# Weight decoding with a one-source 16-bit shift, reordered first loads and last tile, and a new planned order

## The chip, the cores and the metric

One core of one Trainium2 chip runs the whole program. The metric is the device time of one launch in microseconds (us). The runs of the kernel before took 1172.53, 1173.43 and 1179.7 us; their median, 1173.43 us, is the time before.

## The reference: attention, then two dense blocks

The inputs are q, k and v of shape (4, 12, 448, 64) in float32, two gain vectors, and four weight matrices in float64.

```
q_n = q / sqrt(mean(q*q) + 1e-6) * g_q        # the same for k with g_k
attn = softmax(q_n @ k_n^T / sqrt(64))
x = (attn @ v), heads joined                   # 1792 x 768
h = x @ w_in;   x = (h * sigmoid(1.702 h)) @ w_out         # 768 -> 2048 -> 768
h = x @ w_in2;  out = (h * clip(h + 3, 0, 6) / 6) @ w_out2 # 768 -> 2048 -> 768
```

[...] 

## The kernel before: tiles, stages and who sets the order

The work has these stages. For each of the four batches: normalise q and k, turn them (a transposing DMA), scores, exponentials, the product with v; then the first block's input product (`add_in1`) and output product (`add_out1`). The normalising and attention of a batch (`add_norm`, `add_units`) run beside the first block of the batch before it. After the four batches the second block runs over two chunks of 896 tokens in visits (`Quad`, `Visit`); the sum of the output is kept in `acc` and stored in the last visit of each chunk.

The order within each engine's queue is not written by hand. Each step is an `op` with a duration, its dependences and the engines that could do it; `Plan.order` simulates the engines with these durations and picks, for each engine, the ready step of highest rank. `CFG` holds the planner's numbers: biases between engines, look-ahead, offsets of the rank by group of steps, spacing of loads (`pw`, `pu`, `pv`), and `abias`, a penalty in ns that a DMA pays in the choice between the queue of ScalarE (ACT) and that of SyncE (SP). The emitted queues are in order: an instruction that waits holds what is behind it.

Decoding a piece of weight (`Weight.decoded`, line 550, for the first block; `Units.add`, line 703, for the second). A float64 is two 32-bit words. Four steps after its load:

- `sign`, on POOL (GpSimd), lines 578 and 722: the high word, read as float32, is multiplied to a signed zero, which leaves the sign bit in the result.
- `decode_a`, on DVE (VectorE), lines 585 and 728: the low word shifted right by 29 is or-ed into the result. It reads two tensors, in 32-bit words.
- `rebias`, on POOL or ACT, lines 569, 574, 734 and 739: the high word times 2^-112, in place.
- `decode_b`, on DVE, lines 592 and 743: the high word shifted left by 3 is or-ed into the result.

A piece is 128x768 words (W1 and both weights of the second block) or 128x1024 (W2). There are 60 `decode_a`: 16 for W1, 12 for W2 and 32 for the second block.

The start: `gains()` (line 510) is emitted before the planned order. It loads g_q and g_k on SP, sets constants on POOL and computes the joint gain on DVE (lines 518 to 524). The plan then begins with the loads of q and k, the squares (line 921), sums (924), the root (953 to 968), the gain on k (927), the norms (978), the float16 parts (984, 466, 996, 999) and the transposes (1022). The first tile of v for `add_head0` (line 1072) is loaded over the place of g_q, so its load waits until line 518 has read it.

The end: `Visit.leave` (line 1731) does 24 matmuls for one tile of 128 tokens, alternating between its two halves of 384 columns, then adds each half to `acc` on DVE (line 1749), and two DMAs store 64 rows each (line 1763).

Of the kernel before, what the change touches and what calls it, by code (L numbers as in the profile page):

```python
# [13 lines left out]
I64 = mybir.dt.int64  # L14
AF = mybir.ActivationFunctionType
# [18 lines left out]
    bias=[3440, 0, 1020, 1120, 7840],  # L34
    pw=[418, 636, 204686, 5498710540],
    pn=[8287, 2708, 4378, 1393],
    ps=[2095, 0, 1428, 193],
# [4 lines left out]
    look=[60, 250, 0, 0, 200],  # L42
    off=[-975, 86366, 127438, 91083, -33011, 29732, -19700, 94471, -29918, 18727, -18701, -18103, 48010, -34477, -678250, -4593, -16054, -152410, 41835, 254511],
    abias=1455,
    cuts=[],
    bias0=[680, 0, 510, 0, 6780],
    bias1=[4840, 1020, 6000, 730, 1800],
    dlook=1671,
    warm=9,
    late=789,  # L50
    idle=1000,
    pu=10770,
    pmost=5,
    pv=0,
    early_k=[0, 0, 0, 0],
    beside=0.9,
)
# [104 lines left out]
class Plan:  # L162
# [3 lines left out]
    def op(self, ways, deps=(), takes=None, gives=None, dma=None):  # L166

        if isinstance(ways, tuple):
            ways = [ways]
        o = Op(ways, deps, takes, gives, dma)  # L170
        o.key, o.off, o.bias = len(self.ops), self.off, self.bias
        self.ops.append(o)
        return o
# [37 lines left out]
    def order(self):  # L211
# [3 lines left out]
        dma_free = gen_free = seq_free = begun = 0.0  # L215
# [10 lines left out]
        for _ in self.ops:  # L226
            best = None
            for e in range(5):
                can = []
                for o in wait[e]:  # L230
                    r = o.ready[e]
                    if o.takes:
                        free_at = [l.ring.when(l, sum(m.ring is l.ring for m in o.takes[:i])) for i, l in enumerate(o.takes)]
                        if None in free_at:
                            continue
                        r = max([r] + [f[0] + CFG['late'] * (e == PE) for f in free_at])
                    if o.dma and len(o.ways) > 1:
                        r = max(r, dma_free - o.dma[2] - CFG['dlook'])
                    if len(o.ways) > 1:
                        ends = {w[0]: max(seq_free if o.dma and w[0] == ACT else free[w[0]], o.ready[w[0]], r) + w[1]  # L240
                                + (CFG['abias'] * (w[0] == ACT) if o.dma else o.bias[w[0]]) for w in o.ways}
                        if ends[e] > min(ends.values()):
                            continue
                    can.append((max(seq_free if o.dma and e == ACT else free[e], r), -o.rank, o.key, o))
                if can:
                    soon = min(can)[0] + LOOK[e]
                    c = min((c for c in can if c[0] <= soon), key=lambda c: c[1:3])
                    if best is None or c[:3] < best[0]:
                        best = (c[:3], c[3], e)
# [67 lines left out]
def attention_moe_moe_kernel(ctx, tc, q, k, v, g_q, g_k, w_in1, w_out1, w_in2, w_out2, out):  # L317
# [183 lines left out]
    gm, ge = small(), small()  # L501
# [8 lines left out]
    def gains():  # L510
        nc.sync.dma_start(out=gq_t, in_=g_q.unsqueeze(0).to_broadcast([128, D]))
        nc.sync.dma_start(out=gp, in_=g_k.unsqueeze(0).to_broadcast([128, D]))
        nc.gpsimd.memset(one, 1.0)
        make_identity(nc, ident)
        nc.gpsimd.tensor_copy(ident16, ident)
        for i in range(4):
            nc.gpsimd.memset(carve(gt, 7168 + 5376 * i, [128, 21, 128], F16)[:, 14:21, D:128], 0.0)
        nc.vector.tensor_tensor(out=gp, in0=gp, in1=gq_t, op=ALU.mult)
        nc.vector.tensor_reduce(out=gm, in_=gp, axis=AX.X, op=ALU.max, apply_absolute_value=True)
        exponent(ge, gm)  # L520
        nc.vector.reciprocal(gm, ge)
        nc.vector.tensor_scalar_mul(gp, gp, gm)
        nc.vector.tensor_single_scalar(out=alpha, in_=ge, scalar=2.0 ** -25, op=ALU.mult)
        nc.vector.tensor_single_scalar(out=nalpha, in_=ge, scalar=-(2.0 ** -25), op=ALU.mult)


    class Weight:
# [22 lines left out]
        def decoded(self, src, raw, cl):  # L550
# [21 lines left out]

            def rebias_act():
                nc.scalar.activation(out=high(), in_=high(), func=AF.Copy, scale=2.0 ** -112)

# [5 lines left out]

            def decode_a():
# [111 lines left out]
    class Units:  # L694
# [8 lines left out]
        def add(self, q, after, free):  # L703
# [7 lines left out]
            for j in range(2):  # L711
# [14 lines left out]
                def decode_a(cj=cj, wide=wide):  # L726
                    cu = cj.bitcast(U32)
                    nc.vector.scalar_tensor_tensor(
                        out=cu, in0=wide(U32)[:, :, 0], scalar=29, in1=cu,
                        op0=ALU.logical_shift_right, op1=ALU.bitwise_or,  # L730
                    )

                def rebias_pool(high=high):
                    nc.gpsimd.tensor_scalar(
                        out=high(), in0=high(), scalar1=2.0 ** -112, scalar2=1.0, op0=ALU.mult, op1=ALU.mult
# [23 lines left out]
                if self.wide:  # L759
                    x = op((POOL, t_pool(n), sign), [o] + ends[:1], takes=None if j else lease)  # L760
                    x = op((DVE, t_dve_bits(n), decode_a), [x])
                    o = op([(POOL, t_pool(n), rebias_pool), (ACT, t_act(n), rebias_act)], [x])
# [130 lines left out]
    def add_norm(bt, after):  # L893
# [8 lines left out]
        def sums_of(n):  # L902
# [13 lines left out]
            for i, src in ((0, q), (1, k)):  # L916
# [24 lines left out]
                if i:  # L941
                    bt.gained = op(two(gain), [o])
# [87 lines left out]
        for grp in groups:  # L1030
# [3 lines left out]
                (DVE, 1900, lambda n=grp[0], m=m: root(n, m)), sum((p[1] for p in parts), [])  # L1034
# [29 lines left out]
    def add_head0(bt, n, h, pieces, deps):  # L1064
# [5 lines left out]
        for p0, j0, j1, t0, t1, step in ((0, 0, 3, 0, 5, 2), (64, 0, 3, 1, 6, 2), (64, 3, 4, 6, 7, 1)):  # L1070
# [3 lines left out]
            loads.append(sp(64 * (j1 - j0) * 512, load, loads[:1], takes=None if loads else raw_l, wide=False))  # L1074
# [614 lines left out]
    class Visit:  # L1689
# [18 lines left out]
        def enter(self, tb, banks, some):  # L1708
# [3 lines left out]
            for i in some:  # L1712
                f = (0, 2, 1, 3)[i]

                def emit(i=i, f=f):
                    g = self.gview()
                    for j, (ge, we) in enumerate(((0, 0), (0, 1), (1, 0))):
                        for h in range(2):
# [8 lines left out]
                    (PE, t_mm(half, 6), emit), [last[0], W4.done[q]] + [self.done[f, s] for s in sides],  # L1727
                    takes=None if i else banks,
                )

        def leave(self, tb, acc_free, banks=None):
# [3 lines left out]
            if banks is None:  # L1735
                banks = [Lease(mm_ring, 1, True, both=not i) for i in range(2)]
                self.enter(tb, banks, (0, 1))
            self.enter(tb, banks, (2, 3))
            self.left_ = [last[0]]
            ends = []  # L1740
            for h in range(2):
# [11 lines left out]
                if part == 0:  # L1753
                    o = op((ACT, t_act(half, 1), first), [last[0], self.sized] + acc_free, gives=banks[h])
                else:
                    o = op((DVE, t_add(half), add), [last[0], added[at, h]], gives=banks[h])
                added[at, h] = o
                ends.append(o)
            if part == PARTS - 1:
                for i in range(2):  # L1760
                    def store(i=i):
                        b_, t = divmod(2 * at + i, TB)
                        queue().dma_start(out=orow[b_, t], in_=acc[64 * i:64 * i + 64, at])

                    sp(64 * DM * 4, store, ends, wide=False)
# [17 lines left out]
    b0 = batches[0]  # L1783
    off(0)
    add_norm(b0, [])
# [116 lines left out]
    with tc.manual_schedule():  # L1902
        gains()
# [41 lines left out]
```

## Time and profile before

| | before |
|---|---|
| median of 3 runs | 1173.43 us |
| the profiled execution | 1179.83 us |
| its span, first to last instruction | 1178.0 us |
| mean granted TensorE clock | 0.986 |
| busy: PE, DVE, ACT, POOL | 1078.3, 859.4, 716.3, 318.3 us |

PE is TensorE's matmuls, DVE VectorE, ACT ScalarE, POOL GpSimd, SP SyncE, which issues DMAs. A share of busy time is a mean over stages that are bound by different engines, so the rows below are mostly cut by stage. The matmuls of the profile overlap, and their ends are modelled.

### The profile page before, as it was taken

To read this page: it belongs to the slowest core of one execution; us is meant where nothing else is said; L and a number is where in the kernel's file an instruction comes from. 1 tells how busy PE (TensorE), PEld (TensorE's weight loads), DVE (VectorE), ACT (ScalarE), POOL (GpSimd) and SP (SyncE) were. 2 spreads that over 40 slices of the span, in tenths; PEclk is the share of its full clock that TensorE was granted. 3 is DMA by queue.
4 is the path that set the end of the run, shared out by engine and by line. 5 is a ranking of instruction groups with operands and counts; after the bars stand their busy time and mean duration, and the time that the engine had idled before them with its cause. 6 is when DMAs were issued, how large, how long until landed. Compare 5 with 4: busy or idle time off the path is not lost.

```text
span 1178.0 us, 18000 instructions
## 1 busy us (share of the span) xinstructions
PE 1078.3 (92%) x6590; PEld 594.2 (50%) x6590; DVE 859.4 (73%) x1497; ACT 716.3 (61%) x1507; POOL 318.3 (27%) x280
## 2 busy tenths in 40 slices
PE   2788898779989999999989999989999999999998
PEld 0555543345544455545545555445555555555554
DVE  6988889999879866598666888693648855935342
ACT  3989768888767989679885655463545332622210
POOL 5867735444423100140000324340002101100000
PEclk9899999979999999999999999999999999999999
DMA  6886477989758997689975427613423351213033
GB/s 170 202 222 164 157 200 203 186 190 264 148 155 220 193 200 154 153 217 192 194 154 137 158 76 262 223 67 150 127 92 108 107 165 32 76 51 114 1 87 101
DMA packets 236552, 178.88 MB, mean 152 GB/s; under 512 B 194864, under 2 KB 220208, under 8 KB 234928
## 3 DMA queue, kind: packets, MB, share of 16 engines
q1 hardware_dynamic: 227008, 160.86, 54.1%
q10 hardware_dynamic: 9456, 16.88, 4.8%
q8 instruction: 51, 0.84, 0.3%
q14 instruction: 37, 0.30, 0.1%
HBM read 97.88 MB, written 34.41 MB: 112 GB/s over the span
## 4 chain that ended last, share of the span: by engine, by line
PE 44%; DVE 22%; ACT 14%; DMA 11%; issue 5%; POOL 2%; SPq 1%; ACTq 0%; DVEq 0%; POOLq 0%
PE s L1604 8%; PE mm L1719 8%; PE s L1719 7%; PE mm L1604 6%; PE mm L1428 5%; PE mm L1360 5%; ACT p L1166 5%; DMA xt<-p 4%; DMA p<-in_v_dram 4%; DVE p L481 3%; ACT p L466 2%; DVE smalls L1161 2%; DVE gt L481 2%; PE mm L1081 2%; DVE smalls L924 2%
## 5 line engine op out<-in xcount | busy, mean ns | idle before, releaser
L1360 PE MATMUL mm<-xt,wa 128*128 128x448 f16 x1152 | 226.1, 354 | 7.3 <-DVE st L1409 4.1
L1428 PE MATMUL mm<-gt,wb 128*128 128x448 f16 x1152 | 226.2, 353 | 0.0
L1719 PEld LDWEIGHTS <-gt 128*128 128x128 f16 x1344 | 131.9, 98 | 98.7 <-issue 10.7
L1360 PEld LDWEIGHTS <-wa 128*128 128x128 f16 x1152 | 112.8, 99 | 111.0 <-issue 9.9
L1428 PEld LDWEIGHTS <-wb 128*128 128x128 f16 x1152 | 111.7, 98 | 104.1 <-issue 1.4
L1604 PEld LDWEIGHTS <-xt 128*128 128x128 f16 x1008 | 98.6, 98 | 94.6 <-issue 5.0
L1166 ACT ACTIVATE p<-s,smalls 128x448 f32<-128x448 f32 x168 | 120.8, 720 | 14.4 <-DVE p L481 5.2
L1604 PE MATMUL s<-wa,xt 128*128 128x448 f16 x621 | 122.6, 352 | 2.7 <-DVE st L1619 1.5
L481 DVE SCALAR_TENSOR_TENSOR p<-p,smalls 128x448 f16<-128x448 f32 x108 | 78.1, 749 | 25.9 <-ACT p L466 25.5
L1153 PE MATMUL s<-gt 128*128 128x448 f16 (+1 forms) x192 | 61.9, 366 | 37.0 <-ACT p L1166 35.6
L1161 DVE TENSOR_REDUCE smalls<-s 128x2 f32<-128x896 f32 (+1 forms) x96 | 91.7, 964 | 1.2 <-PE s L1156 1.1
L466 ACT ACTIVATE p<-p,smalls 128x448 f16<-128x448 f32 (+2 forms) x119 | 75.6, 669 | 22.2 <-DMA xt<-p 11.2
L1604 PE MATMUL mm<-wa,xt 128*128 128x448 f16 x387 | 76.6, 352 | 1.9 <-ACT wb L1626 1.9
L1719 PE MATMUL mm<-p,gt 128*128 128x384 f16 x372 | 72.3, 326 | 0.0
L722 POOL TENSOR_SCALAR wr<-wr 128x768 f32<-128x768 f32 x16 | 19.9, 1241 | 169.7 <-DVE xt L687 134.2
L1719 PE MATMUL s<-p,gt 128*128 128x384 f16 x300 | 61.0, 326 | 4.1 <-ACT wb L1626 2.6
L1719 PE MATMUL s<-gt 128*128 128x384 f16 x324 | 58.7, 333 | 3.4 <-DVE wb L1749 2.4
L1156 PE MATMUL s<-gt 128*128 128x448 f16 (+1 forms) x192 | 61.6, 362 | 0.0
L1719 PE MATMUL mm<-gt 128*128 128x384 f16 x348 | 60.8, 326 | 0.0
L1114 PE MATMUL mm<-xt,gt 128*64 128x64 f16 (+3 forms) x858 | 51.6, 265 | 4.3 <-DMA xt<-p 3.6
L1215 PE MATMUL mm<-gt,p 128*128 128x128 f32 x336 | 46.1, 293 | 9.5 <-ACT xt L1225 4.1
L481 DVE SCALAR_TENSOR_TENSOR gt<-st,smalls,gt 128x448 f16<-128x448 f32 x64 | 51.2, 808 | 4.5 <-ACT gt L466 4.2
(212 smaller groups left out, 1808.7 us busy)
## 6 DMA issues: line engine op xcount, KB each, us to landing
wr<-in_moe_w_in_dram SPq DMA_DIRECT2D x27, 768.0 KB, 4.9
wa<-park_x SPq DMA_DIRECT2D x21, 672.0 KB, 4.0
wr<-in_moe_w_out_dram SPq DMA_DIRECT2D x16, 768.0 KB, 4.5
qkd<-xt SPq DMA_DIRECT2D x18, 672.0 KB, 5.1
wr<-in_moe_w_out_dram SPq DMA_DIRECT2D x8, 1024.0 KB, 5.4
p<-in_v_dram SPq DMA_DIRECT2D x36, 224.0 KB, 3.8
park_x<-wa SPq DMA_DIRECT2D x2, 2688.0 KB, 12.1
out_dram<-wb SPq DMA_DIRECT2D x28, 192.0 KB, 2.6
```

Source lines behind the costliest of these rows:

```text
L466: nc.scalar.activation(out=dst(), in_=src(), func=AF.Copy, scale=s)
L481: nc.vector.scalar_tensor_tensor(out=dst(), in0=src(), scalar=s, in1=high(), op0=ALU.mult, op1=ALU.subtract)
L1114: nc.tensor.matmul(mm_t[ml.slot][64 * h:64 * h + 64, c:c + m * w], lhsT=vhl[:, 2 * (i % 4) + i // 4, part], rhs=pt[:, s:s + w, i, q0:q0 + ...
L1153: nc.tensor.matmul(o, lhsT=x[:, 64 * t:64 * t + m], rhs=x[:, 448:896], start=True, stop=False)
L1156: nc.tensor.matmul(o, lhsT=x[:, 64 * t:64 * t + m], rhs=x[:, 896:1344], start=False, stop=True)
L1161: nc.vector.tensor_reduce(out=nb, in_=s_t[sl.slot][:, :m, :S], axis=AX.X, op=ALU.max)
L1166: nc.scalar.activation(out=p(i), in_=s_t[sl.slot][:, i, :S], func=AF.Exp, bias=nb[:, i:i + 1], scale=alpha, accum_out=z[:, i:i + 1],)
L1215: nc.tensor.matmul(mm_t[tl.slot][:, 128 * j:128 * j + 128], lhsT=p(i)[:, c:c + 128], rhs=diag(), start=True, stop=True,)
L1360: nc.tensor.matmul(mm_t[ml.slot][:, :n], lhsT=w.inw(we, kc, f), rhs=x[:, xe, kc, :n], start=(kc == k0 and i == 0), stop=(kc == k1 - 1 and ...
L1428: nc.tensor.matmul(mm_t[ml.slot][:, :S], lhsT=W2.outw(we, fc, d * 128, 128), rhs=gv[:, ge_, fc, :], start=(fc == g.part.start and i == 0), ...
L1604: nc.tensor.matmul(self.bank(k), lhsT=w[:, we, fa, kc], rhs=xs[:, fb, xe, kc], start=first and kc == 0 and j == 0, stop=kc == 2 and j == 2 ...
L1719: nc.tensor.matmul(mm_t[banks[h].slot][:, :half], lhsT=g[:, ge, f, tb * 128:tb * 128 + 128], rhs=w4_t[part % 2][:, f, we, h * half:h * hal ...
```

## The change

`decode_a` becomes a shift of 16-bit words: of the four 16-bit words of a float64 it takes the second lowest, shifts it right by 13, and writes the low 16-bit word of each result. It reads one tensor, no longer the result. The value is the same, since the step `sign` has left zeros there. `sign` may now also be a 16-bit "and" on DVE, and `rebias` may also run on DVE; the planner chooses. The planner's duration for `decode_a` goes from 1.04 n + 150 ns to 0.72 n + 80 ns.

`gains()` is split. Constants are still emitted first. A one-element `Exp` on ACT comes first in the plan (`table`). The loads of g_q and g_k are planned DMAs, the arithmetic is a planned DVE step, and the gain on k and the first v load name it as a dependence. In the last tile of the last visit each half of 384 columns does its 12 matmuls by itself, is added as soon as its own are done, and is stored by two DMAs of its own (four of 64x384). The planner's numbers are new, `abias` goes from 1455 to 44617, its DMA model starts at 4800 ns, and a table `own` shifts the rank of some 80 single steps.

```diff
-    look=[60, 250, 0, 0, 200],
-    off=[-975, 86366, 127438, ...
-    abias=1455,
+    look=[0, 130, 60, 920, 540],
+    off=[-9158, 408922, -29895, ...
+    abias=44617,
...
-    pu=10770,
+    pu=419,
...
+    own={
+        1: 18285, 2: 13033, 4: 14353, 7: 16590, 17: 60615, 21: 15124, 23: 56483, 26: 34835, 28: 63794, 29: 27563,
...
+    def constants():
         nc.gpsimd.memset(one, 1.0)
         make_identity(nc, ident)
...
+    def table():
+        nc.scalar.activation(out=tab, in_=one, func=AF.Exp)
+
+    def load_gq():
+        queue().dma_start(out=gq_t, in_=g_q.unsqueeze(0).to_broadcast([128, D]))
+
+    def load_gk():
+        queue().dma_start(out=gp, in_=g_k.unsqueeze(0).to_broadcast([128, D]))
...
+    def low16(c):
+        return c.bitcast(U16).rearrange("p (n t) -> p n t", t=2)[:, :, 0]
+
+    def high16(c):
+        return c.bitcast(U16).rearrange("p (n t) -> p n t", t=2)[:, :, 1]
+
+    def last16(raw):
+        return raw.bitcast(U16).rearrange("p (n t) -> p n t", t=4)[:, :, 3]
+
+    def next16(raw):
+        return raw.bitcast(U16).rearrange("p (n t) -> p n t", t=4)[:, :, 1]
...
+            def sign_dve():
+                nc.vector.tensor_single_scalar(
+                    out=high16(c32()), in_=last16(wr_t[raw.slot][:, :n]), scalar=0x8000, op=ALU.bitwise_and
+                )
+
             def decode_a():
 
-                cu = c32().bitcast(U32)
-                nc.vector.scalar_tensor_tensor(
-                    out=cu, in0=wide(U32)[:, :, 0], scalar=29, in1=cu,
-                    op0=ALU.logical_shift_right, op1=ALU.bitwise_or,
+                nc.vector.tensor_single_scalar(
+                    out=low16(c32()), in_=next16(wr_t[raw.slot][:, :n]), scalar=13, op=ALU.logical_shift_right
                 )
...
-                x = op((POOL, t_pool(n), sign), [o], takes=cl)
-                x = op((DVE, t_dve_bits(n), decode_a), [x])
-                o = op([(POOL, t_pool(n), rebias_pool), (ACT, t_act(n), rebias_act)], [x])
+                x = op([(POOL, t_pool(n), sign), (DVE, t_fast(n), sign_dve)], [o], takes=cl)
+                x = op((DVE, t_fast(n), decode_a), [x])
+                o = op([(POOL, t_pool(n), rebias_pool), (ACT, t_act(n), rebias_act), (DVE, t_fast(n), rebias_dve)], [x])
...
-                    bt.gained = op(two(gain), [o])
+                    bt.gained = op(two(gain), [o] + with_gains)
...
-            loads.append(sp(64 * (j1 - j0) * 512, load, loads[:1], takes=None if loads else raw_l, wide=False))
+            loads.append(sp(64 * (j1 - j0) * 512, load, loads[:1] or with_gains, takes=None if loads else raw_l, wide=False))
...
+            final = self.turn + 1 == len(order) and tb + 1 == 2 * self.n // 128
+            made = [None, None]
+            if final:
+                banks = [Lease(mm_ring, 1, True) for _ in range(2)]
+                for h in range(2):
+                    self.enter(tb, banks, range(4), [h])
+                    made[h] = last[0]
...
-                for i in range(2):
-                    def store(i=i):
+                for i in range(4 if final else 2):
+                    def store(h=i // 2, i=i % 2):
                         b_, t = divmod(2 * at + i, TB)
...
+    op((ACT, 1400, table)).off = 1e9
     off(0)
+    with_gains = [op((DVE, 1500, gains), [sp(128 * 256, load_gq, wide=False), sp(128 * 256, load_gk, wide=False)])]
...
     with tc.manual_schedule():
-        gains()
+        constants()
         plan.run()
```

The second block's decoding is changed in the same way, with the same four new steps.

## Rows read from the trace of the kernel before

**Rows 1.** Page, part 1: busy us (share of the span) and instructions of each engine.

```profile
PE 1078.3 (92%) x6590; PEld 594.2 (50%) x6590; DVE 859.4 (73%) x1497; ACT 716.3 (61%) x1507; POOL 318.3 (27%) x280
```

**Rows 2.** Windows by stage: length, then busy us of PE, PEld, DVE, ACT, POOL; clock, DMA.

```profile
0.00:20.40 20.40, 0.00 (x0) 0.00 (x0) 11.56 (x34) 6.54 (x11) 9.95 (x19) 1.00 0.55 189
20.40:60.00 39.60, 30.68 (x168) 18.27 (x169) 38.21 (x61) 31.34 (x80) 33.72 (x30) 0.90 0.85 189
60.00:152.00 92.00, 77.70 (x553) 51.51 (x552) 76.07 (x123) 77.05 (x203) 66.56 (x57) 0.99 0.63 179
...
176.00:300.00 124.00, 102.12 (x645) 52.92 (x644) 118.98 (x198) 103.67 (x233) 56.84 (x41) 0.93 0.92 210
...
365.00:640.00 275.00, 265.17 (x1808) 140.79 (x1806) 202.49 (x395) 222.69 (x534) 36.87 (x38) 1.00 0.84 183
...
740.00:800.00 60.00, 53.24 (x296) 28.67 (x295) 46.06 (x83) 32.78 (x51) 22.73 (x20) 1.00 0.43 150
...
905.00:945.00 40.00, 37.56 (x211) 21.09 (x210) 32.30 (x50) 16.15 (x24) 6.79 (x6) 0.96 0.31 99
```

**Rows 3.** Waits of PE in 150 to 300 us: us in total, times, longest.

```profile
PE s L1153 <- ACT p L1166: 18.6, 11, 5.1
```

**Rows 4.** Timeline of the first 20 us: start, duration, engine, line, operation.

```profile
0.74 0.41 ACTq L918 DMA_DIRECT2D wb<-in_q_dram  x1
...
6.64 0.23 DVE L518 TENSOR_TENSOR gp<-gp,p 128x64 f32<-128x64 f32 x1 [6.64 <-DMA gp<-in_g_k_dram]
6.90 0.71 ACTq L1072 DMA_DIRECT2D p<-in_v_dram  x1
...
7.64 1.28 ACT L921 ACT_TABLE_LOAD   x1 [7.64 <-DVE smalls L440]
...
8.94 2.91 ACT L921 ACTIVATE gt<-wb 128x448 f32<-128x448 f32 x6
```

**Rows 5.** DMA issues: queue, count, size, median us to landing.

```profile
wb<-in_k_dram ACTq DMA_DIRECT2D x2, 224.0 KB, 5.1
wb<-in_q_dram ACTq DMA_DIRECT2D x1, 224.0 KB, 4.8
...
gp<-in_g_k_dram SPq DMA_DIRECT2D x1, 32.0 KB, 5.4
```

**Rows 6.** Instructions of lines 585 and 728: ns min/median/max, first and last start, form.

```profile
L585 DVE SCALAR_TENSOR_TENSOR wb<-wr,wb x16: 943/958/1654, 26.9 to 127.0; 128x768 uint32<-128x768 uint32 x16
L585 DVE SCALAR_TENSOR_TENSOR wr<-wr x12: 1210/1218/2162, 136.4 to 300.3; 128x1024 uint32<-128x1024 uint32 x12
...
L728 DVE SCALAR_TENSOR_TENSOR wr<-wr x16: 942/951/960, 329.2 to 993.8; 128x768 uint32<-128x768 uint32 x16
```

**Rows 7.** One-source DVE instructions, lines 469 and 956, the same view.

```profile
L469 DVE TENSOR_SCALAR xt<-wr,smalls x5: 1012/1016/1020, 635.3 to 983.6; 128x1536 f16<-128x1536 f32 x5
...
L469 DVE TENSOR_SCALAR gt<-st,smalls x1: 453/453/453, 549.2 to 549.2; 128x448 f16<-128x448 f32 x1
...
L956 DVE TENSOR_SCALAR smalls<-smalls x13: 177/183/1055, 11.3 to 522.8; 128x28 int32<-128x28 int32 x11, 128x14 int32<-128x14 int32 x2
```

**Rows 8.** Windows, line 585 alone, then line 728: length, DVE busy (count), clock, DMA.

```profile
20.40:60.00 39.60, 5.78 (x5) 0.90 0.85 189
60.00:152.00 92.00, 14.02 (x13) 0.99 0.63 179
...
176.00:300.00 124.00, 14.13 (x9) 0.93 0.92 210
...
740.00:800.00 60.00, 3.81 (x4) 1.00 0.43 150
...
905.00:945.00 40.00, 3.79 (x4) 0.96 0.31 99
```

**Rows 9.** Issues of the v loads of line 1095 by ACT's queue.

```profile
L1095 ACTq DMA_DIRECT2D p<-in_v_dram x23: 602/612/1015, 170.7 to 618.8; - x23
```

**Rows 10.** Timeline of the last 6 us.

```profile
1172.60 1.14 DVE L1749 SCALAR_TENSOR_TENSOR wb<-mm,smalls,wb 128x384 f32<-128x384 f32 x2 [2.60 <-PE mm L1719]
```

More of the change, by code (lines that the diff above doesn't have):

```diff
@@ L33 @@
 CFG = dict(
[L34 to L37, printed above, removed]
+    bias=[2580, 340, 2500, 1380, 5660],
+    pw=[847, 1827, 3991690324, 32301064499],
+    pn=[78, 1413, 6578, 11344],
+    ps=[1104, 851, 1934, 2727],
     rw=[2, 2, 3, 5],
@@ L170, in op @@
         o = Op(ways, deps, takes, gives, dma)
-        o.key, o.off, o.bias = len(self.ops), self.off, self.bias
+        o.key, o.off, o.bias = len(self.ops), CFG['own'].get(len(self.ops), 0.0) + self.off, self.bias
         self.ops.append(o)
@@ L235, in order @@
                             continue
[L236 removed]
+                        r = max([r] + [f[0] + (CFG['late'] + o.slack) * (e == PE) for f in free_at])
                     if o.dma and len(o.ways) > 1:
@@ L759, in add @@
                 if self.wide:
-                    x = op((POOL, t_pool(n), sign), [o] + ends[:1], takes=None if j else lease)
-                    x = op((DVE, t_dve_bits(n), decode_a), [x])
-                    o = op([(POOL, t_pool(n), rebias_pool), (ACT, t_act(n), rebias_act)], [x])
+                    x = op([(POOL, t_pool(n), sign), (DVE, t_fast(n), sign_dve)], [o] + ends[:1], takes=None if j else lease)
+                    x = op((DVE, t_fast(n), decode_a), [x])
+                    o = op([(POOL, t_pool(n), rebias_pool), (ACT, t_act(n), rebias_act), (DVE, t_fast(n), rebias_dve)], [x])
                     o = op((DVE, t_dve_bits(n), decode_b), [o])
@@ L1033, in add_norm @@
             rooted = op(
-                (DVE, 1900, lambda n=grp[0], m=m: root(n, m)), sum((p[1] for p in parts), [])
+                (DVE, 2300, lambda n=grp[0], m=m: root(n, m)), sum((p[1] for p in parts), [])
             )
@@ L1717, in emit @@
                     for j, (ge, we) in enumerate(((0, 0), (0, 1), (1, 0))):
-                        for h in range(2):
+                        for h in sides_:
                             nc.tensor.matmul(
@@ L1726, in enter @@
                 last[0] = op(
-                    (PE, t_mm(half, 6), emit), [last[0], W4.done[q]] + [self.done[f, s] for s in sides],
-                    takes=None if i else banks,
+                    (PE, t_mm(half, 3 * len(sides_)), emit), [last[0], W4.done[q]] + [self.done[f, s] for s in sides],
+                    takes=None if i else [banks[h] for h in sides_],
                 )
@@ L1753, in leave @@
                 if part == 0:
-                    o = op((ACT, t_act(half, 1), first), [last[0], self.sized] + acc_free, gives=banks[h])
+                    o = op((ACT, t_act(half, 1), first), [made[h], self.sized] + acc_free, gives=banks[h])
                 else:
-                    o = op((DVE, t_add(half), add), [last[0], added[at, h]], gives=banks[h])
+                    o = op((DVE, t_add(half), add), [made[h], added[at, h]], gives=banks[h])
                 added[at, h] = o
@@ L1759, in leave @@
             if part == PARTS - 1:
-                for i in range(2):
-                    def store(i=i):
+                for i in range(4 if final else 2):
+                    def store(h=i // 2, i=i % 2):
                         b_, t = divmod(2 * at + i, TB)
-                        queue().dma_start(out=orow[b_, t], in_=acc[64 * i:64 * i + 64, at])
-                    sp(64 * DM * 4, store, ends, wide=False)
+                        cols = slice(h * half, h * half + half) if final else slice(None)
+                        queue().dma_start(out=orow[b_, t][:, cols], in_=acc[64 * i:64 * i + 64, at, cols])
+                    sp(64 * DM * 4, store, ends[i // 2:i // 2 + 1] if final else ends, wide=False)
     def cycle(u, prev, between=lambda: None):
```

49 lines of the change are left out of this document (31 added, 18 removed), and 8 rows, old and new, of the table own.

## The prediction

> **What bounds the kernel now.** I read the page's busy shares first. PE is busy 1078.3 us of a span of 1178.0 [rows 1], so about 100 us of PE idleness is all that a change of order or of the other engines can win. Next I cut the span by stage to see where that idleness lies and which engine is full there [rows 2]. Length minus PE busy gives 20.4 us before the first matmul, 8.9 in 20.4 to 60, 14.3 in 60 to 152, 21.9 in 176 to 300, 9.8 in 365 to 640, 6.8 in 740 to 800 and 2.4 in 905 to 945. The mean DVE share of 73% hides this: DVE is 96.5% busy in 20.4 to 60 (38.21 of 39.60) and 96.0% in 176 to 300 (118.98 of 124.00). In these two stretches DVE sets the pace; PE mostly waits there for score buffers that ACT's exponentials release [rows 3], and those in their turn wait for maxima that stand in DVE's queue. From 365 to 640 and after 800 PE is nearly full, and a shorter DVE step buys little. The third view is the start [rows 4]: the first square begins only at 8.94, behind a table load at 7.64, behind the issue of a v load on ACT's queue at 6.90, which had to wait until line 518 had read g_q (6.64 + 0.23 us).
>
> **The shift, per instruction.** The old step takes 0.958 us for 768 words and 1.218 for 1024 when nothing disturbs it [rows 6]; the means with disturbance are 14.13/9 = 1.57 in 176 to 300 and 5.78/5 = 1.16 in 20.4 to 60 [rows 8]. The trace has no 16-bit shift. Its nearest rows are one-source instructions from SBUF to SBUF: 448 elements take 0.453, 1536 take 1.016 [rows 7], a slope of 0.563/1088 = 0.517 ns per element. By interpolation 768 elements take 0.62 us and 1024 take 0.75. Against that stands the other end: the new step reads every fourth and writes every second 16-bit word, and if that costs it the fast rate, it is as slow as the old one. I take 0.62 and 0.75, because those rows too are one-source and large.
>
> Gain per instruction, undisturbed: 0.34 us for 768, 0.47 for 1024. Upper end, if the disturbance goes too: 0.54 and 0.82 in the two full stretches.
>
> [...]
>
> **What of it reaches the end.** Each stretch by its count [rows 8]:
> - 20.4 to 60, five steps, DVE full: between 5 x 0.34 = 1.7 and 5.78 - 5 x 0.62 = 2.7; I take 2.2.
> - 60 to 152, thirteen steps (eleven of 768, two of 1024): 14.02 - 8.3 = 5.7 us of DVE at most. DVE is 83% busy there, with ACT at 84% and PE at 84%, so no engine alone decides. I take a third, 2; bounds 0 and 5.7.
> - 176 to 300, nine steps, DVE full: between 9 x 0.47 = 4.2 and 14.13 - 9 x 0.75 = 7.4; I take 6. ACT, next with 103.67 us, leaves room for that.
> - The second block, 32 steps, 32 x 0.34 = 10.9 us of DVE. Only the four in 740 to 800 and the four in 905 to 945 stand where PE idles: at most 2.7, I take 2. PE's matmuls hide the rest; if that cover goes, up to 8 us more count.
>
> **Start.** With the table loaded first (1.28 us, while q is still in flight) the first square can begin when q lands: issue at 0.74 plus 4.8 = 5.5, instead of 8.94 [rows 4, 5]. That is 3.4 us at most. The k square needs k, issued at 1.18, plus 5.1 = 6.3. The moved arithmetic is seven DVE instructions from 6.64 to about 8.1, and its two loads now stand in SP's queue with those of q and k. If all four are issued there at some 0.45 us each, g_k is issued near 2.1 and lands near 7.5 (5.4 to landing), and the arithmetic ends near 9. The added wait is the gain on k, on POOL, and behind it the k norm; today that gain starts at about 10, so it is not later. Also in DVE's queue the arithmetic may stand ahead of the first sums. I take 2.5 us; bounds 0 (g_q and g_k first, or q behind other loads) and 3.4. The constants on POOL stay where they were.
>
> **Tail.** Today both adds (1.14 us) follow the last matmul [rows 10]. Afterwards the first half's add lies beside the second half's matmuls: 0.57 us less. The last two stores are half as large but as many. I take 0.6; bounds 0.3 and 1.2. Matmuls and weight loads are as many as before.
>
> **Order.** `abias` takes nearly all DMAs from ACT's queue to SP's: an issue of a v tile there takes 0.61 us, 23 times [rows 9]. Which steps change places can't be read from the diff. Of the 64 us of idleness named above between 20.4 and 945 I give it 3, for the weight loads of 905 to 945, which a shorter spacing (`pu`) lets start earlier, since there PE waits 2.4 us and the clock falls to 0.96 [rows 2]. Bounds: 20 lost, 20 won.
>
> **Sum.** 2.2 + 2 + 6 + 2 + 2.5 + 0.6 + 3 = 18.3 us. The profiled execution took 1179.83 us, 1178.0 of span and 1.8 around it; it is 6.4 us above the median of 1173.43, and I take the saving from the median: 1155 us.
>
> **Rivals.**
> 1. [...] The shift may be held by POOL as the old step is. A one-source step of line 956 took 1.055 us where its median is 0.183 [rows 7], beside a POOL instruction; the old shift ranges to 2.16 [rows 6]. POOL is busy 85% of 20.4 to 60 and 46% of 176 to 300 [rows 2]. If a held shift ends when POOL's instruction ends, whatever its own length, the gains shrink to 15%, 28% (60 to 152) and 54%: 0.3, 0.6 and 3.2 instead of 2.2, 2 and 6, so 6.1 less: 1161. Against it: the minimum of the old step is also its median, so most were not held. [...] Chance 0.13.
> 2. *No fast rate.* The step at 0.95 us: 12 us of the sum go, and 1167 is left. For it: no row shows a strided 16-bit step. Chance 0.10.
> 3. *SP's queue.* The 23 v issues alone are 23 x 0.61 = 14 us on SP, in front of the transposes of the attention. If half of that delays a transpose that PE waits for, 7 us return: 1162. Chance 0.07.
> 4. *More from the order.* If it also returns a third of the 45 us of PE idleness in 20.4 to 60, 60 to 152 and 176 to 300, 15 us more go: 1140. For it: no engine is full in 60 to 152. Chance 0.15.
> 5. *Slower: DVE takes over sign and rebias.* In 176 to 300 nine pieces have eighteen such steps; on DVE each costs 0.75. From eight of them on (8 x 0.75 = 6) the gain of 6 there is gone. All eighteen cost 13.5, net 7.5; ten in 20.4 to 60 at 0.62 cost 6.2, net 4; eight in 740 to 945 cost 5, net 3. With the 3.1 of start and tail against that, and nothing from the order: 1173.4 + 14.5 - 3.1 = 1185. For it: the planner may choose DVE. Against it: its bias for DVE is not below POOL's in most groups (2500 against 1380, 3900 against 3250). Chance 0.10.
>
> **Numbers.** The forecast has the remaining 0.45; its own range is 1145 to 1161. A change of 1% (11.7 us) is about what measurement can tell from no change. Faster by more, below 1161.7: the forecast, rival 4 and half of rival 1, 0.67. Slower by more: rival 5, 0.10. Within: 0.23. The range from 1136 to 1172 leaves out rival 5 and about half of rival 4.
>
> **What would show it.** The shift at 0.55 to 0.8 us in its row; line 921's first square near 5.5; DVE's share in the stretch of W2's decoding below 96% and PE's idleness there below 15 us; one add, not two, after the last matmul. I am wrong if the shift's row stands at 0.95, if new DVE rows for sign or rebias number more than about twenty before 300 us, or if SP's issues reach the transposes later.

## The result, and the profile after

The changed kernel takes 1147.43 us (median of four runs, 1146.72 to 1148.28); the kernel before, run beside it, 1175.98 (1172.53 to 1179.7). The ratio is 0.9756, with a 95% interval of 0.973 to 0.9781: 2.4% faster. The profiled execution took 1147.63 us, 1145.8 of it span. The forecast of 1155 lies 7.6 us above the median. It was taken from a median of 1173.43 for the kernel before; against that the changed kernel is 26.0 us faster, against 1175.98 it is 28.6.

Part 1 of the page of the changed kernel, busy us (share of the span) and instructions, against [rows 1]:

```profile
PE 1065.3 (93%) x6571; PEld 588.7 (51%) x6571; DVE 822.5 (72%) x1445; ACT 721.3 (63%) x1505; POOL 365.1 (32%) x335
```

DVE lost 37 us of work, POOL gained 47. PE has 19 instructions fewer, all of them filler matmuls (55 before, 36 after), products without use that the planner puts in where PE would stand idle. The same windows as in [rows 2]: length, then busy us of PE, PEld, DVE, ACT, POOL; clock, DMA.

```profile
0.00:20.40 20.40, 4.14 (x10) 1.49 (x11) 12.46 (x35) 9.48 (x20) 10.59 (x19) 1.00 0.73 227
20.40:60.00 39.60, 32.70 (x206) 20.49 (x205) 38.27 (x69) 35.35 (x90) 28.28 (x30) 1.00 0.96 213
60.00:152.00 92.00, 78.47 (x561) 52.44 (x560) 80.10 (x155) 80.43 (x189) 53.56 (x55) 1.00 0.64 180
176.00:300.00 124.00, 108.21 (x722) 56.62 (x721) 112.44 (x196) 114.54 (x254) 54.27 (x45) 0.92 0.90 203
365.00:640.00 275.00, 268.23 (x1823) 142.20 (x1822) 196.15 (x366) 215.40 (x515) 56.96 (x54) 0.99 0.78 170
...
905.00:945.00 40.00, 40.00 (x229) 22.23 (x228) 17.97 (x34) 10.15 (x14) 0.56 (x1) 1.00 0.38 121
```

PE's idleness in 176 to 300 fell from 21.9 to 15.8 us and DVE's share from 96.0% to 90.7%, nearly as forecast (below 15 us, below 96%). But the work has moved: the same window now holds a later part of the program, so these rows can't price a part of the change. For that I cut both spans at the same points of the program: the first scores, the last product of probabilities and v of the first batch, the first output product of the first block, the last product of probabilities and v of the fourth batch, the first and the last input product of the second block (the expectations below call it gate-and-up). The kernel before:

```profile
24.80:148.10 123.30, 100.47 (x689) 66.47 (x689) 106.95 (x170) 103.07 (x274) 94.71 (x81) 0.96 0.70 184
148.10:251.90 103.80, 82.52 (x477) 42.11 (x477) 96.63 (x181) 78.81 (x168) 44.71 (x35) 0.92 0.87 204
251.90:633.70 381.80, 365.13 (x2457) 194.26 (x2455) 295.07 (x562) 304.82 (x715) 79.81 (x71) 1.00 0.84 185
...
742.70:1121.70 379.00, 366.11 (x2070) 202.73 (x2069) 235.30 (x372) 155.76 (x233) 51.17 (x44) 1.00 0.29 97
```

The changed kernel, the same points:

```profile
24.90:133.20 108.30, 97.26 (x697) 65.98 (x698) 100.52 (x182) 99.80 (x247) 68.48 (x75) 1.00 0.72 186
133.20:237.80 104.60, 77.46 (x452) 39.34 (x452) 94.03 (x174) 82.62 (x172) 54.41 (x44) 0.85 0.85 212
237.80:611.30 373.50, 361.56 (x2447) 191.20 (x2445) 280.10 (x528) 305.70 (x721) 101.84 (x93) 1.00 0.84 190
...
721.80:1090.30 368.50, 362.00 (x2063) 201.74 (x2062) 225.49 (x354) 152.74 (x232) 78.19 (x63) 1.00 0.30 100
```

I call these stages attention 1, attention 2, the first block (with the attention of the later batches beside it) and the second block. With the start, the rest of the first block in front of the second, and the tail they went from 24.8, 123.3, 103.8, 381.8, 109.0, 379.0, 56.3 to 24.9, 108.3, 104.6, 373.5, 110.5, 368.5, 55.5 us. So the time came from attention 1 (15.0), the first block (8.3) and the second (10.5), and nothing from attention 2, where the forecast had its largest term. About 4 us of the second block are scatter: two kernels below with the old order there have 374.9 and 375.4. A stage read from one execution is not sharper than some 2 us. In the profiles of experiments 5 and 10, whose queues up to 720 us are those of the changed kernel, attention 1 took 109.0 and 110.8 us (108.3 above), attention 2 102.9 and 103.6 (104.6), the first block 374.0 and 372.4 (373.5); the second block took 370.3 in experiment 5 (368.5).

The shift's own rows, against [rows 6] (ns min/median/max, first and last start, form):

```profile
L628 DVE TENSOR_SCALAR wb<-wr x16: 584/609/1390, 13.0 to 116.8; 128x768 uint16<-128x768 uint16 x16
L628 DVE TENSOR_SCALAR wr<-wr x12: 730/743/989, 127.0 to 294.2; 128x1024 uint16<-128x1024 uint16 x12
...
L774 DVE TENSOR_SCALAR wr<-wr x16: 591/606/1314, 325.1 to 967.2; 128x768 uint16<-128x768 uint16 x16
```

The interpolated 0.62 and 0.75 us are 0.609 and 0.743. The start, against [rows 4] (start, duration, engine, line, operation):

```profile
0.74 1.28 ACT L531 ACT_TABLE_LOAD   x1 [0.74 <-PEq L1980]
...
4.55 0.58 ACT L971 ACTIVATE gt<-wb 128x448 f32<-128x448 f32 x1 [2.31 <-DMA wb<-in_k_dram]
...
7.71 0.23 DVE L540 TENSOR_TENSOR gp<-gp,p 128x64 f32<-128x64 f32 x1 [1.93 <-DMA gp<-in_g_k_dram]
```

The first square starts at 4.55 instead of 8.94, and yet the first scores start at 24.95 instead of 24.8.

### The profile page after: what moved, and what is told of

Same layout as the page of the kernel before. It is cut to its first block, busy times and chain, and to the rows that moved or that the text cites. A ratio compares the mean times of both kernels' runs of the same rounds, so it can differ in the third digit from the quotient of the medians.

```text
span 1145.8 us, 18018 instructions
## 1 busy us (share of the span) xinstructions
PE 1065.3 (93%) x6571; PEld 588.7 (51%) x6571; DVE 822.5 (72%) x1445; ACT 721.3 (63%) x1505; POOL 365.1 (32%) x335
## 5 line engine op out<-in xcount | busy, mean ns | idle before, releaser
L1410 PE MATMUL mm<-xt,wa 128*128 128x448 f16 x1152 | 229.5, 357 | 7.0 <-DVE st L1459 6.8
L1654 PE MATMUL s<-wa,xt 128*128 128x448 f16 x576 | 114.1, 352 | 2.1 <-DVE st L1669 2.1
L1654 PE MATMUL mm<-wa,xt 128*128 128x448 f16 x432 | 86.9, 352 | 0.9 <-ACT wb L1676 0.9
L1769 PE MATMUL mm<-gt 128*128 128x384 f16 x372 | 68.2, 326 | 0.0
L1769 PE MATMUL s<-p,gt 128*128 128x384 f16 x288 | 56.1, 326 | 2.4 <-ACT wb L1805 1.2
L1769 PE MATMUL s<-gt 128*128 128x384 f16 x300 | 55.9, 326 | 1.0 <-DVE st L1669 0.6
L1808 DVE SCALAR_TENSOR_TENSOR wb<-mm,smalls,wb 128x384 f32<-128x384 f32 x47 | 27.0, 611 | 41.0 <-PE mm L1769 41.0
L479 ACT ACTIVATE gt<-st,smalls 128x448 f16<-128x448 f32 x49 | 32.1, 661 | 29.9 <-DVE st L1459 26.2
```

The lines of the kernel that those rows point to most:

```text
L479: nc.scalar.activation(out=dst(), in_=src(), func=AF.Copy, scale=s)
L1410: nc.tensor.matmul(mm_t[ml.slot][:, :n], lhsT=w.inw(we, kc, f), rhs=x[:, xe, kc, :n], start=(kc == k0 and i == 0), stop=(kc == k1 - 1 and ...
L1654: nc.tensor.matmul(self.bank(k), lhsT=w[:, we, fa, kc], rhs=xs[:, fb, xe, kc], start=first and kc == 0 and j == 0, stop=kc == 2 and j == 2 ...
L1769: nc.tensor.matmul(mm_t[banks[h].slot][:, :half], lhsT=g[:, ge, f, tb * 128:tb * 128 + 128], rhs=w4_t[part % 2][:, f, we, h * half:h * hal ...
L1808: nc.vector.scalar_tensor_tensor(out=view(), in0=bank(), scalar=self.co, in1=view(), op0=ALU.mult, op1=ALU.add)
```

## The experiments

Each is one edit. "Stage" is a stretch as cut above, from the profile of that kernel; the kernel before ran beside each.

**1. The shift alone, in the old order.**

```
 kernel before, every queue in its old order:
-    scalar_tensor_tensor(out=cu, in0=wide, scalar=29, in1=cu, op0=shift_right, op1=or)
+    tensor_single_scalar(out=low16(c), in_=next16(raw), scalar=13, op=shift_right)
```

> The kernel before with its queues exactly as they were; only the 60 decode_a instructions are the 16-bit shift. Theory A (the prediction's: shorter DVE steps in the two stretches where DVE is full move the end, wherever the order puts them): 12 us less, a ratio of about 0.990, most of it between 148 and 252 us. Theory B (the new order is what won; in a fixed order the shift's time turns into other waits): at most 4 us less, ratio 0.997 or above. In both the shift's median is about 0.60 us for 768 words and 0.74 for 1024.

Measured: 1171.98 us, ratio 0.9943 (0.9915 to 0.9971), so 3 to 10 us. Stages: 120.0, 102.3, 384.9, 374.2 (from 123.3, 103.8, 381.8 and some 375). Attention 1 gives 3.3 us, attention 2 only 1.5; the first block is 3.1 longer, of which scatter can be a part (383.4 and 382.5 in experiments 4 and 8). Theory A's 12 us lie outside the interval, theory B's 4 inside.

**2. The old operation in the new order.**

```
 changed kernel, every queue in its new order:
-    tensor_single_scalar(out=low16(c), in_=next16(raw), scalar=13, op=shift_right)
+    scalar_tensor_tensor(out=cu, in0=wide, scalar=29, in1=cu, op0=shift_right, op1=or)
 (the 7 sign steps on DVE as an f32 product of the same shape)
```

> The changed kernel with its queues exactly as they are, but decode_a is the old two-source 32-bit instruction again. Theory A: some 12 us longer than the changed kernel, ratio to the kernel before about 0.986. Theory B: at most 5 us longer, ratio about 0.980 or less.

Measured: 1153.74 us, ratio 0.9786 (0.9743 to 0.9829): theory A's 0.986 lies outside, theory B's 0.980 inside. Against the changed kernel that is 6.3 us by the medians and 3.5 by the two ratios, so the 6.3 is not sharper than some 3 us. Its stages (windows, columns as above):

```profile
24.40:137.90 113.50, 98.84 (x697) 67.42 (x698) 107.61 (x183) 101.32 (x249) 73.34 (x76) 0.98 0.69 180
137.90:243.40 105.50, 77.39 (x452) 39.27 (x452) 98.87 (x175) 82.79 (x172) 56.05 (x44) 0.85 0.84 212
243.40:617.00 373.60, 359.77 (x2445) 190.94 (x2444) 284.13 (x528) 306.15 (x721) 102.11 (x93) 1.00 0.82 189
...
727.50:1097.60 370.10, 362.10 (x2065) 201.40 (x2063) 232.65 (x354) 153.25 (x232) 78.89 (x63) 1.00 0.31 102
```

Read from these two profiles, the shift is worth 5.2 us in attention 1, 0.9 in attention 2, 0.1 in the first block, 1.6 in the second. Only the first is clear of scatter: against the stages of experiments 5 and 10 as well it is 2.7 to 5.2, attention 2 0.9 to 2.6, and the 1.6 vanishes (370.1 here, 370.3 in experiment 5). Everything else of the change without the shift takes some 22 us off (1175.98 to 1153.74).

**3. The shift twice.**

```
+    for _ in range(2):
         tensor_single_scalar(out=low16(c), in_=next16(raw), scalar=13, op=shift_right)
```

> The changed kernel with every one of the 60 shifts issued twice, the second time writing the same bits again; nothing else moves. Theory (VectorE's time sets the pace only as long as W1 is decoded; elsewhere TensorE or the waits for ScalarE do): the first attention stage goes from 108.3 to 116 to 119 us (16 more shifts of 0.6 us, 9.6 us), the stage of 104.6 by at most 3 us (5 of W2's 12 shifts lie in it, 3.7 us), the stage of 373.5 us and the second block by at most 2 us each, though 7 and 32 more shifts (5 and 19 us) lie there. Rival (VectorE sets the pace in W2's stage and in the second block as the forecast had it): 4 us or more in the stage of 104.6, 4 us or more in the second block.

Measured: 1164.83 us, ratio 0.9884 (0.9849 to 0.9919), 17 us above the changed kernel. Stages:

```profile
24.90:143.20 118.30, 101.67 (x698) 68.61 (x698) 112.31 (x199) 101.43 (x249) 69.03 (x75) 0.96 0.66 171
143.20:250.30 107.10, 78.02 (x452) 39.48 (x453) 101.19 (x179) 82.99 (x172) 55.90 (x44) 0.84 0.81 206
250.30:626.10 375.80, 361.56 (x2447) 191.68 (x2445) 286.35 (x536) 306.58 (x721) 101.52 (x94) 1.00 0.82 189
736.60:1108.70 372.10, 363.40 (x2063) 202.08 (x2062) 235.71 (x374) 153.12 (x232) 77.34 (x63) 1.00 0.31 102
```

In attention 1 the 16 added shifts (14 x 0.634 + 2 x 0.754 = 10.4 us by their medians here) cost 10.0 us: nearly the full price. In attention 2 five cost 2.5 of 3.8, in the first block eight cost 2.3 of 5.7, in the rest of the first block ten cost nothing of 6, in the second block twenty cost 3.6 of 12.2. The last is 1.6 more than expected against the one profile of the changed kernel; against the 370.3 of experiment 5 it is 1.8 in all, as expected. The rival's 4 us in attention 2 and in the second block did not come.

**4. Most of the start alone, in the old order.**

```
-    gp, gq_t = sb.tile([128, D], F32, name="gp"), vr_t[0][:, 0, :]
+    gp, gq_t = sb.tile([128, D], F32, name="gp"), st_t[NST - 1][:, :D]
...
+            if o.way[0] == ACT:
+                sent += 1
+                if sent == 2:
+                    self.table()
```

> The kernel before in its own order, with two things of the start changed: g_q has a place of its own, so that the first v load on ACT's queue does not wait for line 518, and the table is loaded right after the issue of the first q and k loads. The first square should begin near 5.6 us instead of 8.94. Theory A: 2.5 us less, ratio 0.998, and the first scores 2 to 3 us earlier. Theory B (the start of the chain is given back before the scores, as in the changed kernel, where the first scores start at 24.9 against 24.8 us): no difference.

Measured: 1177.18 us, ratio 0.9982 (0.9954 to 1.0011). The first square came at 5.36 and the first scores 1.1 us earlier (23.7) in the profile; of that nothing can be told in the time. The interval holds both theories, and the 2 to 3 us at the first scores of theory A did not come.

**5. The tail undone.**

```
-            final = self.turn + 1 == len(order) and tb + 1 == 2 * self.n // 128
+            final = False
```

> The changed kernel, but the last tile ends as before: both halves' last matmuls, then both adds. Theory (the split is worth what its one add costs): two adds of about 0.7 us follow the last matmul instead of one, and the last stage (from the last gate-and-up matmul of the second block to the end, 55.5 us) comes to 56.2 to 56.4, all other stages as in the changed kernel (24.9, 108.3, 104.6, 373.5, 110.5, 368.5), each within 2 us. Rival (the four half-width stores at the end cost as much as the add saves): 55.5 again.

Measured: 1149.12 us in one run, and the last stage 56.3 instead of 55.5: the split is worth the 0.8 us of the stage. The kernels below and above without the split have 56.3 or 56.4 there, those with it 55.4 to 55.8. In the changed kernel one add of 0.62 us follows the last matmul.

**6. The new code with the planner's old numbers.**

```
 changed kernel: CFG's 12 changed numbers and lists as before
+    own={},
```

> All code of the change, planned with the planner's numbers of the kernel before and without single offsets. Theory A: the shift and the start stay, the numbers' 3 to 15 us go: 1155 to 1165 us, ratio 0.985 to 0.993. Theory B: nearly the whole gain goes, 1168 to 1178 us, ratio 0.995 to 1.003.

Measured: 1195.52 us, ratio 1.0123 (1.0069 to 1.0178): slower than before, and both theories missed. Under the old numbers the new code gains nothing; why this plan is so much slower stays open (attention 2 takes 115.2 us in it instead of 103.8).

**7. The DMA issues back on ScalarE.**

```
         for o in self.done:
+            if o.dma and o.key in on_act:        # the 63 that ACT issued before
+                o.way = next(w for w in o.ways if w[0] == ACT)
             o.way[2]()
```

> The changed kernel, with the same order of everything, but the 63 DMAs that ScalarE's queue issued in the kernel before are issued by it again, each at its place in the order. Theory A (ScalarE freed of 63 issues of about 0.6 us, 38 us of its sequencer, is a main part of what the order gained): 10 to 20 us slower than 1147, most of it where ScalarE is fullest, the stages of 373.5 us (to 378 to 383) and 108.3 us (to 111 to 115). Rival B (which engine does the vector work is what counts): within 3 us of 1147, every stage within 2 us.

Measured: 1164.02 us, ratio 0.9898 (0.9869 to 0.9928): 16.6 us of the gain are gone. Its stages:

```profile
23.80:140.00 116.20, 98.75 (x698) 67.53 (x698) 100.42 (x184) 100.37 (x248) 68.53 (x75) 0.97 0.69 176
140.00:247.80 107.80, 78.64 (x452) 39.46 (x453) 93.68 (x173) 82.15 (x170) 53.81 (x44) 0.84 0.83 203
247.80:627.10 379.30, 362.10 (x2445) 191.47 (x2444) 279.50 (x528) 307.80 (x722) 101.76 (x93) 1.00 0.82 190
```

No engine is busier than in the changed kernel by more than 2.1 us, and the stages are longer by 7.9, 3.2 and 5.8 us. The size is theory A's, and rival B is out. Attention 1 holds only nine of the 63 issues, which take 32.9 us of ScalarE's queue in all, so the issue time is not all. Waits of PE there (us in total, times, longest; line 1211 here is line 1203 of the changed kernel):

```profile
PE s L1211 <- DMA gt<-gt: 6.4, 2, 5.6
PE s L1211 <- ACT p L1224: 4.7, 7, 1.6
```

The changed kernel waits 1.8 us for these transposes, so they are 4.6 of the 7.9 us; where the rest comes from stays open. A k load that SP issued at 32.92 goes out at 39.56 from ScalarE's queue, behind ScalarE's own work, and the transposes behind it come later (the last at 96.95 instead of 90.38).

**8. The DMA issues moved to SP in the old order.**

```
 kernel before:
         for o in self.done:
+            if o.dma and len(o.ways) > 1:
+                o.way = o.ways[0]                # SP
             o.way[2]()
```

> The kernel before with one thing changed: the 63 DMAs that ScalarE's queue issued are issued by SP, each at its old place in the order. Theory A (ScalarE's time for the issues is a good part of what the order gained, in the old order too): 7 to 15 us faster than before, shared by the first attention stage (123.3 us) and the stage of 381.8 us, the second block as it was. Rival (the old order was laid out for two queues; with one, loads and transposes wait for their turn behind each other): within 4 us of before, or slower.

Measured: 1173.3 us, ratio 0.9962 (0.9934 to 0.9989), 1 to 8 us, below theory A's 7 to 15 except at its upper end, and none of it in attention 1 (124.6 us). The waits of DVE in that stage point to the reason:

```profile
DVE wb L587 <- POOL wb L580: 5.0, 7, 1.4
DVE smalls L1176 <- ACT smalls L1173: 3.9, 4, 2.9
DVE wb L594 <- POOL wr L571: 3.2, 3, 1.7
```

In the old order POOL holds the sign and the rebias of W1 (lines 580 and 571 here) and is busy 96.30 of 124.60 us, while ScalarE's own work there stays as it was (102.82 us, 103.07 in the kernel before). That freed time on ScalarE is of no use as long as POOL has the rebias is my reading of these rows; no run tests it by itself.

**9. The old engines in the new order, and the new engines in the old.**

```
 e9, changed kernel:   271 vector operations to the engine they had before
 e13, kernel before:   264 vector operations to the engine they have now, all DMA issues to SP
+            if o.key in table: o.way = next(w for w in o.ways if w[0] == table[o.key])
             o.way[2]()
```

> The changed kernel with the same order, but each of the 271 vector operations that changed its engine goes back to the engine of the kernel before; DMA issues stay on SP. Theory B (the engines' shares carry the gain of the order, above all GpSimd rid of the W1 rebias that VectorE waited for): 10 to 20 us slower than 1147, with the first attention stage at 116 to 122 us instead of 108.3. Theory A or the order itself: the first attention stage stays within 3 us of 108.3. More than 30 us slower would say that the new order doesn't fit the old shares, and nothing on what they are worth in the old order.

> The kernel before in its own order, with the old operations, but with the changed kernel's choice of engine: the 63 DMAs from SP instead of ScalarE's queue, and 264 vector operations on the engine that the changed kernel gives them (the 7 sign operations that it gives to VectorE stay on GpSimd). Theory (the shares of the engines carry the gain of the order, and freeing ScalarE of DMA issues is worth something only together with giving it the W1 rebias): 1155 to 1163, the first attention stage at 110 to 116 us instead of 123.3 and the stage of 381.8 at 374 to 379. Rival (the sequence carries it; shares and sequence fit only each other): first attention stage at 120 us or more, and 1170 or more in all.

Measured: 1175.07 us for the first, ratio 0.9996 (0.9975 to 1.0017): the whole gain gone, attention 1 at 119.4. And 1201.17 for the second, ratio 1.0184 (1.0123 to 1.0245): with the shares of the faster kernel, the old sequence is slower than it was, attention 1 at 133.5. Waits of POOL in that stage of the second kernel:

```profile
POOL gt L501 <- DVE smalls L1203: 25.0, 7, 6.0
POOL wb L607 <- DMA wr<-in_moe_w_in_dram: 7.4, 5, 4.6
POOL wa L501 <- DVE smalls L484: 5.5, 2, 5.2
```

POOL has been given more of the scaling of the identity by the reciprocals, with which PE transposes the probabilities (line 501), at places in its queue where the reciprocals are late, and W1's sign steps wait behind it. That this is what lengthens the stage is not shown: DVE waits only 1.5 us there for W1's signs and PE 2.3 us for line 501, less than PE's 10.4 us for exponentials. My theory that the shares carry the gain falls; so does the one that the sequence does. Either alone gives nothing or worse.

**10. The old spacing of the second block's loads.**

```
-    pu=419,
+    pu=10770,
-    pv=1315,
+    pv=0,
```

> The changed kernel with the planner's two numbers that space the second block's weight loads and products put back (pu 419 to 10770, pv 1315 to 0); the first difference in any queue lies after 722 us. Theory (the earlier loads of the second block carry its part of the gain): the stretch from the first to the last gate-and-up matmul of the second block goes from 368.5 to 374 to 379 us, TensorE's idle time in it from 6.5 to 10 to 13 us, the whole to 1153 to 1158. Rival (that part of the gain is the order of the vector work there, or scatter): 367 to 371, and 1146 to 1150 in all.

Measured: 1144.77 us, ratio 0.9743 (0.9717 to 0.977), not to be told from the changed kernel (0.973 to 0.9781); the second block 366.0. The theory fails, and in its premise: the loads of W3 that were issued at 868.20 still go out at 865.15, 144 us behind the block's first matmul against 146 (178 in the kernel before). In the new order these two numbers don't set when they go, so whether the earlier loads carry the second block's part stays open.

**11. More filler where the clock is low.** In 168.7 to 196 the changed kernel has a granted clock of 0.50; it fell while PE waited 5.14 us for exponentials. Attention 2 as a whole has a mean of 0.84 or 0.85 there and in experiments 2, 3 and 7, 0.92 in the kernel before.

```
 keep_busy(free[PE], start)
+self.more(free[PE], {585: 12, 978: 7, ...}.get(o.key, 0))   # filler ahead of these waits
```

> The changed kernel with 19 more filler matmuls on TensorE, 12 and 7, ahead of the first two waits of the stretch at 165 to 193 us in which the granted clock is at half and TensorE waits for the exponentials (for the later waits no PSUM bank is free). Theory (the low clock there costs little, since TensorE waits for VectorE and ScalarE anyway): within 2 us of 1147, whether or not the clock stays up longer. Rival (it costs up to half of TensorE's 10.3 us of work in that stretch): if the granted clock of 168.7 to 196 us rises above 0.8, 3 to 5 us faster than 1147.

Measured: 1145.74 us, ratio 0.9729 (0.9703 to 0.9755), not to be told from the changed kernel. That stretch of the changed kernel:

```profile
168.70:196.00 27.30, 10.27 (x29) 3.97 (x30) 26.36 (x49) 22.74 (x51) 13.23 (x11) 0.50 0.92 240
```

and of this one:

```profile
168.70:196.00 27.30, 13.42 (x39) 4.71 (x39) 24.83 (x47) 22.16 (x52) 13.11 (x12) 0.59 0.75 220
```

The clock rose to 0.59 only, short of the 0.8 that I had set as the condition, so what the low clock costs stays open. Attention 2 as a whole took 107.1 us here, no less than without the filler.

## Why the prediction was right, and where it was not

The direction and the size were right, out of terms that were partly wrong. That the time fell into the stated range is in part luck: shift and start were put some 8 us too high, the order some 18 too low.

**The shift's duration** is right, and rival 2 (no fast rate, 0.95 us) is out: 0.609 us for 768 words. Slope and constant can be told apart: (743 - 609)/256 = 0.523 ns per element, against the 0.517 of [rows 7], and 609 - 768 x 0.523 = 207 ns, an estimate from the two medians.

**What of it reaches the end** was mis-sized in one term above all, "176 to 300, nine steps, DVE full", with "I take 6". It measured 0.9 (attention 2; up to 2.6 with the scatter) plus 0.1. The window ended at 300, but the stage ends at 251.9, and the two halves differ. The kernel before, windows:

```profile
176.00:252.00 76.00, 56.41 (x341) 28.72 (x340) 72.46 (x127) 61.49 (x137) 35.15 (x26) 0.89 0.89 202
252.00:300.00 48.00, 45.72 (x306) 24.20 (x305) 46.51 (x72) 42.17 (x96) 21.69 (x15) 1.00 0.96 223
```

Five of the nine steps lie behind 252, where PE is busy 45.72 of 48 us: DVE is full there beside a full PE, and a shorter step buys nothing (the 0.1). The steps of attention 2, four before and five in the changed kernel, got a third to two thirds of their price (0.9 of 3.0 us of DVE in experiment 2, 2.5 of 3.8 in experiment 3). The terms of 20.4 to 152 (2.2 + 2) measured 5.2, since DVE sets the pace through all of attention 1, also where I had called no engine the bound: doubling the shift had nearly its full price there. The second block's 2 measured 1.6, not to be told from scatter. Together 7.8 by the stages and 6.3 by the medians, instead of 12.2.

**The start** (2.5) gave nothing that can be told. Its mechanism was right up to the gains: the first square (of k, which now loads first) at 4.55, earlier than the 5.5 forecast. The failed step is that a time won in the first 9 us would reach the first scores. Other work has taken the place (the first shift of W1 starts at 13.0 instead of 26.9), and the first transposed q and k decide: PE's wait of 1.76 us for them ends at 24.95.

**The tail** (0.6) measured 0.8.

**The order** (3, "for the weight loads of 905 to 945, which a shorter spacing (`pu`) lets start earlier") is worth some 20 us: 28.6 less 6.3 for the shift, 0.8 for the tail and nothing for the start leaves 21.5. The step failed twice: `pu` doesn't move those loads (experiment 10), and the gain comes mostly from attention 1 (9.8 us without the shift) and the first block (8.2), less 1.7 in attention 2 and 1.5 in the rest of the first block. In attention 1 it is DVE's idle time that went: DVE has about the same work in the kernel before and in experiment 2 (106.95 and 107.61 us) and stands idle 16.4 us in the first, 5.9 in the second. Which of the moved steps did that stays open. Rival 4, at 1140, had the right direction; the measured time lies midway between it and the forecast. What makes the gain is ScalarE without DMA issues, the new shares and the new sequence together: putting back the first costs 16.6 us, putting back the second 27.6, and the sum is more than the gain. In the old order the first alone brings some 5, and first and second together lose 24.

**Rival 3** had the sign wrong in the end: in the new order, with the issues off ScalarE's queue, that load and the transposes behind it come earlier (experiment 7). **Rival 5** did not come: DVE takes two sign steps before 300 us and seven in all, and no rebias; the planner gave W1's rebias to ScalarE (line 613, 14 in attention 1, 12.4 us). **Rival 1**: its mechanism is there, its size is not. Twelve of the 60 shifts are held by POOL (last section), three of the sixteen in attention 1 among them (0.98, 1.39 and 1.34 us). But the mean in attention 1 is 11.73/16 = 0.73 where the undisturbed mix is 0.63, so holding takes back 0.1 us each, not most of the gain.

## What to carry to other kernels

A window has to end where the program's stage ends: a full engine beside a waiting TensorE and a full engine beside a full one look alike in a share of 96%, and only the first had a price here, in attention 2 not the full one. Doubling the disputed step and reading the stages gives that price for each stage in one run, as far as it exceeds the 2 us by which a stage scatters. Where a plan chooses engines, queues and sequence together, its parts can't be priced one by one: each alone, put into the other plan, was worth little or cost up to 2%.

## What the runs showed of the hardware

Some DVE instructions that started beside a running POOL instruction were held until that one had ended: of the two kinds read one by one here, 16 of 28 and 12 of 60. The first kind is in the decode, which makes a float32 of each float64 weight and splits it into a high and a low float16 part: the scale-and-subtract that makes the low part of W1 (128 x 768), from the groups by line in attention 1 (count, busy us, mean ns). The kernel before,

```profile
L481 DVE SCALAR_TENSOR_TENSOR wa<-wb,smalls,wa 128x768 f16<-128x768 f32 x14 | 20.5, 1494 | 0.0
```

the changed kernel,

```profile
L494 DVE SCALAR_TENSOR_TENSOR wa<-wb,smalls,wa 128x768 f16<-128x768 f32 x14 | 15.5, 1121 | 0.7 <-POOL wa L485 0.7
```

the old engines in the new order,

```profile
L523 DVE SCALAR_TENSOR_TENSOR wa<-wb,smalls,wa 128x768 f16<-128x768 f32 x14 | 17.6, 1266 | 2.2 <-POOL wa L514 2.2
```

and the new engines in the old order.

```profile
L510 DVE SCALAR_TENSOR_TENSOR wa<-wb,smalls,wa 128x768 f16<-128x768 f32 x14 | 15.4, 1124 | 0.0
```

POOL is busy 94.71 of 123.30 us in the first, 68.48 of 108.30 in the second, 83.00 of 119.40 in the third and 70.53 of 133.50 in the last. The mean follows POOL's share in the same sequence (1494 to 1124, 1266 to 1121), 2 to 5 us over 14 instructions. The single instructions of the kernel before and of the changed kernel show what lengthens it. Of these 28, 16 took 1.12 to 2.39 us; each ended 0.80 to 0.82 us after a POOL instruction that was running when it started (two of these POOL instructions started within 0.02 us of it). The other 12 took 1.00 to 1.05 us, six of them beside a POOL instruction too.

The new shift is held in the same way. Of the 60 in the changed kernel, twelve took longer than the rest of their size (0.76 to 1.39 us); each ended 0.46 to 0.49 us after a POOL instruction that was running when it started (0.62 for the one of 1024 words). The other 48 took 0.58 to 0.62 us (768 words) and 0.73 to 0.76 (1024), also where a POOL instruction started beside them. One of each, from the timeline of the changed kernel (start, duration):

```profile
49.17 1.13 POOL L977 TENSOR_TENSOR wb<-wb,gp 128x448 f32<-128x448 f32 x1
49.38 1.39 DVE L628 TENSOR_SCALAR wb<-wr 128x768 uint16<-128x768 uint16 x1
...
111.54 0.61 DVE L628 TENSOR_SCALAR wb<-wr 128x768 uint16<-128x768 uint16 x1
111.59 0.76 POOL L485 TENSOR_SCALAR gt<-gt,smalls 128x128 f32<-128x128 f32 x1
```

The shift reads one tensor and the scale-and-subtract two, and both are held; why is not shown. The rows also show the limit of this as an explanation of time: the new engines in the old order have the short step (a mean of 1124 ns) and the longest stage (133.50 us).
